# A two-layer feed-forward kernel on one core: the second layer's last token block, its first product run on 256 + 256 or 384 + 128 columns instead of 512

## The chip, the cores and the metric

The kernel runs on one core of a Trainium2 chip. The metric is the device time of one execution in microseconds (us), lower is better. Before the change two executions took 648.00 and 648.39 us, median 648.19 us.

## The reference, cut to what matters

```python
attn_out = _attn_ref(q, k, v, n_sink, window)       # 2 x 8 heads, 768 tokens, 64 wide
x = attn_out.transpose(0, 2, 1, 3).reshape(1536, 512)
# first layer: softplus
h = x @ moe_w_in                                    # 512 -> 2048
x = (np.maximum(h, 0) + np.log1p(np.exp(-np.abs(h)))) @ moe_w_out
# second layer: hard swish
h = x @ moe2_w_in
g = h * np.clip(h + 3.0, 0.0, 6.0) / 6.0
return g @ moe2_w_out                               # 1536 x 512
```

The weights and the attention inputs arrive as 64-bit floats; the result is 32-bit.

## The kernel before

First comes a windowed attention (`banded_attention`, about the first 120 us), which leaves its result transposed in the tile `xT` (128 partitions, a high and a low part, 4 slices of the 512 features, 1536 tokens). Then come the two layers, `w1` (softplus) and `w2` (hard swish). Each layer goes through three token blocks (`blk` 0, 1, 2 of 512 tokens), and each block through 16 slices `c` of 128 hidden features. In all that is 2 x 3 x 16 = 96 steps.

A step has three parts. `products` (lines 136 to 152) makes the tile `h` of one step, 128 hidden features by 512 tokens, in a PSUM tile of pool `psa` (three tiles in turn): for each of the 4 slices of x's features it issues three matrix products, weights high by x high, weights high by x low, weights low by x high, so 12 MATMULs (line 144), each with its own loading of 128 weight columns (LDWEIGHTS, also listed under line 144). `activate` turns h into g; for `w2` that is a Relu on ScalarE (line 178), a product on VectorE (line 180), the high part on ScalarE (line 181) and the low part on VectorE (line 182). `stage_b` (line 201) multiplies g with w_out, again 12 MATMULs in a step (four tiles `y`, three products each), and after the last slice `evac` copies the four y tiles out (lines 218 and 220) and stores them.

All operands of lines 144 and 201 are of the type float32r; the profile prints this type and plain float32 both as "f32" in matrix products. The matrix products of the attention are plain float32: a transposition (lines 525 and 589) shows as one loading and one product, the other ones (lines 483, 552 and 567) as two of each per call in the program. Line 603 are products of zeros in bfloat16 that keep TensorE busy at the start.

`run` issues step s's first products and activation, and then the second product of step s - 2. The first four steps stand in the order in which they are written; from there on (`ffn.run(FIXED, 1000)`) a scheduler sets the order of each engine's instructions, from a model of its own of how long each takes. The second products of the very last two steps are issued tile by tile, each waiting for the one before.

In names of tiles in the rows below the layer's digit is left out: `h_w` is any of `h_w1_...` and `h_w2_...`.

Of the kernel before, what the change touches and what calls it, by code (L numbers as in the profile page):

```python
# [18 lines left out]
P = 128  # L19
# [99 lines left out]
class Ffn:  # L119
# [16 lines left out]
    def products(self, key, blk, c):  # L136
        nc, xT = self.nc, self.xT
        wt = self.w.parts[key, c, 0]
        t0 = blk * 512
        h = self.psa.tile([P, 512], F32, tag="s", name=f"h_{key}_{blk}_{c}")  # L140
        n = 0
        for kk in range(4):
            for ws, xs in ((0, 0), (0, 1), (1, 0)):
                nc.tensor.matmul(  # L144
                    h,
                    wt[:, ws, kk * P : (kk + 1) * P],
                    xT[:, xs, kk, t0 : t0 + 512],
                    start=(n == 0),
                    stop=(n == 11),
                )  # L150
                n += 1
        self.h[key, blk, c] = h

    def activate(self, key, kind, blk, c, filler):
# [641 lines left out]
```

## Time and profile before

| | |
|---|---|
| median of two executions | 648.19 us (648.00 and 648.39) |
| span of the profiled execution, first to last instruction | 646.4 us |
| TensorE busy | 635.6 us, 98% of the span |
| VectorE, ScalarE, GpSimd busy | 335.9, 333.3 and 215.8 us |
| granted TensorE clock, mean over the span | 0.999 of 2.4 GHz |

The profile gives the profiled execution by its span; no separate total is listed for it, so the 1.8 us between the span and the median of the two executions are taken as what lies around it. A busy time counts the stretches in which at least one instruction of an engine was under way. MATMULs overlap, so the time that one costs is the distance from its start to the next start, not the length of its record.

### The profile page before, as it was taken

To read this page: it belongs to the slowest core of one execution; us is meant where nothing else is said; L and a number is where in the kernel's file an instruction comes from. 1 tells how busy PE (TensorE), PEld (TensorE's weight loads), DVE (VectorE), ACT (ScalarE), POOL (GpSimd) and SP (SyncE) were. 2 spreads that over 40 slices of the span, in tenths; PEclk is the share of its full clock that TensorE was granted. 3 is DMA by queue.
4 is the path that set the end of the run, shared out by engine and by line. 5 is a ranking of instruction groups with operands and counts; after the bars stand their busy time and mean duration, and the time that the engine had idled before them with its cause. 6 is when DMAs were issued, how large, how long until landed. Compare 5 with 4: busy or idle time off the path is not lost.

```text
span 646.4 us, 8792 instructions
## 1 busy us (share of the span) xinstructions
PE 635.6 (98%) x3148; PEld 523.0 (81%) x3148; DVE 335.9 (52%) x693; ACT 333.3 (52%) x707; POOL 215.8 (33%) x197
## 2 busy tenths in 40 slices
PE   8999999999999999999999999999999999999996
PEld 4898787878888888888888888888888888888884
DVE  4788989599922422225899987222232222322221
ACT  3777777578866756667777864222222222222221
POOL 1113123489964444445798964000000000000000
PEclk9999999999999999999999999999999999999999
DMA  7744572650000000004665731000010000100001
GB/s 205 236 135 144 164 243 81 233 209 1 1 1 1 0 2 1 1 7 132 189 193 171 219 100 34 1 1 0 2 65 1 0 1 1 65 1 0 1 1 70
DMA packets 38141, 47.06 MB, mean 73 GB/s; under 512 B 2120, under 2 KB 30792, under 8 KB 38088
## 3 DMA queue, kind: packets, MB, share of 16 engines
q1 hardware_dynamic: 37400, 46.15, 22.6%
q8 instruction: 26, 0.43, 0.3%
q10 hardware_dynamic: 688, 0.26, 0.2%
q14 instruction: 27, 0.22, 0.1%
HBM read 43.26 MB, written 3.15 MB: 72 GB/s over the span
## 4 chain that ended last, share of the span: by engine, by line
PE 88%; issue 5%; DVE 3%; ACT 2%; POOL 1%; POOLq 0%; ACTq 0%; DVEq 0%
PE y_w L201 39%; PE h_w L144 39%; PE o L567 3%; PE s L483 2%; PE pt L525 2%; PE spare L603 1%; PE o L552 1%; ACT P L500 1%; POOL w_w L107 1%; DVE xs L495 0%; PE xtr L589 0%; DVE t_w L102 0%; DVE e_w L174 0%; DVE PT L538 0%; POOL ring L460 0%
## 5 line engine op out<-in xcount | busy, mean ns | idle before, releaser
L144 PE MATMUL h_w<-xT,w_w 128*128 128x512 f32 x1152 | 281.9, 389 | 0.8 <-DVE e_w L174 0.8
L144 PEld LDWEIGHTS h_w<-xT,w_w 128*128 128x128 f32 x1152 | 215.9, 188 | 46.7 <-DVE e_w L174 1.3
L201 PE MATMUL y_w<-g_w,w_w 128*128 128x512 f32 x576 | 142.6, 389 | 0.0
L201 PE MATMUL y_w<-w_w,g_w 128*128 128x512 f32 x576 | 138.9, 389 | 0.0
L201 PEld LDWEIGHTS y_w<-w_w,g_w 128*128 128x128 f32 x576 | 108.0, 188 | 23.2 <-ACT g_w L181 0.4
L201 PEld LDWEIGHTS y_w<-g_w,w_w 128*128 128x128 f32 x576 | 108.1, 188 | 22.5
L107 POOL TENSOR_TENSOR w_w<-t_w,w_w 128x512 fp32r<-128x512 f32 x64 | 82.9, 1297 | 44.7 <-ACT w_w L106 44.3
L180 DVE SCALAR_TENSOR_TENSOR h_w<-e_w,h_w 128x512 f32<-128x512 f32 x48 | 33.4, 696 | 89.0 <-ACT e_w L178 89.0
L178 ACT ACTIVATE e_w<-h_w 128x512 f32<-128x512 f32 x48 | 28.7, 599 | 96.2 <-PE h_w L144 94.6
L176 POOL TENSOR_TENSOR g_w<-e_w,g_w 128x512 fp32r<-128x512 f32 x48 | 62.2, 1297 | 43.9 <-ACT g_w L175 43.9
L182 DVE SCALAR_TENSOR_TENSOR g_w<-h_w,g_w 128x512 fp32r<-128x512 f32 x48 | 33.2, 691 | 84.0 <-ACT g_w L181 84.0
L181 ACT ACTIVATE g_w<-h_w 128x512 fp32r<-128x512 f32 x48 | 28.7, 598 | 91.4 <-PE y_w L201 91.1
L170 POOL TENSOR_TENSOR u_w<-u_w,e_w 128x512 f32<-128x512 f32 x48 | 62.1, 1295 | 34.4 <-ACT u_w L169 33.6
L500 ACT ACTIVATE P<-xs,mx 128x272 f32<-128x272 f32 (+1 forms) x96 | 47.3, 494 | 31.8 <-DVE mx L495 31.7
L173 DVE SCALAR_TENSOR_TENSOR h_w<-h_w,r_w 128x512 f32<-128x512 f32 x48 | 33.4, 696 | 58.1 <-ACT r_w L171 58.1
L166 ACT ACTIVATE e_w<-h_w 128x512 f32<-128x512 f32 x48 | 28.4, 592 | 45.5 <-PE h_w L144 39.9
L174 DVE TENSOR_TENSOR e_w<-h_w,u_w 128x512 f32<-128x512 f32 x48 | 33.0, 688 | 28.8 <-POOL u_w L170 28.5
L567 PE MATMUL o<-v,PT 128*128 128x64 f32 x352 | 45.0, 271 | 1.5 <-DVE PT L538 1.3
L106 ACT ACTIVATE w_w<-t_w 128x512 fp32r<-128x512 f32 x64 | 40.0, 625 | 12.6 <-DVE t_w L102 11.7
L567 PEld LDWEIGHTS o<-v,PT 128*128 128x128 f32 x352 | 42.7, 191 | 3.0 <-DVE PT L538 1.9
L96 DVE TENSOR_SCALAR m_w<-raw_w 128x512 int32<-128x512 int32 x52 | 36.1, 693 | 7.5 <-DMA raw_w<-in_moe_w_in_dram 3.6
L175 ACT ACTIVATE g_w<-e_w 128x512 fp32r<-128x512 f32 x48 | 29.9, 624 | 17.4 <-DVE e_w L174 13.6
(80 smaller groups left out, 523.1 us busy)
## 6 DMA issues: line engine op xcount, KB each, us to landing
raw_w<-in_moe_w_in_dram SPq DMA_DIRECT2D x32, 512.0 KB, 5.1
raw_w<-in_moe_w_out_dram SPq DMA_DIRECT2D x32, 512.0 KB, 3.7
v<-in_v_dram SPq DMA_DIRECT2D x12, 256.0 KB, 5.3
out_dram<-o SPq DMA_DIRECT2D x12, 256.0 KB, 2.4
q<-in_q_dram SPq DMA_DIRECT2D x11, 256.0 KB, 3.0
ring<-in_k_dram SPq DMA_DIRECT2D x11, 256.0 KB, 3.8
ring<-in_k_dram ACTq DMA_DIRECT2D x2, 128.0 KB, 6.1
q<-in_q_dram SPq DMA_DIRECT2D x2, 128.0 KB
```

The source lines that it names most:

```text
L96: nc.vector.tensor_scalar(out=m, in0=hi, scalar1=3, scalar2=0x3FFFFFF8, op0=ALU.logical_shift_left, op1=ALU.bitwise_and)
L106: nc.scalar.activation(wt[:, 0, :], t.bitcast(F32), AF.Copy)
L107: nc.gpsimd.tensor_tensor(out=wt[:, 1, :], in0=t.bitcast(F32), in1=wt[:, 0, :].bitcast(F32), op=ALU.subtract)
L144: nc.tensor.matmul(h, wt[:, ws, kk * P : (kk + 1) * P], xT[:, xs, kk, t0 : t0 + 512], start=(n == 0), stop=(n == 11),)
L170: nc.gpsimd.tensor_tensor(out=u, in0=u, in1=e, op=ALU.subtract)
L173: nc.vector.scalar_tensor_tensor(out=h, in0=h, scalar=0.0, in1=r, op0=ALU.max, op1=ALU.add)
L176: nc.gpsimd.tensor_tensor(out=glo, in0=e, in1=ghi.bitcast(F32), op=ALU.subtract)
L180: nc.vector.scalar_tensor_tensor(out=h, in0=e, scalar=6.0, in1=h, op0=ALU.min, op1=ALU.mult)
L182: nc.vector.scalar_tensor_tensor(out=glo, in0=h, scalar=1.0 / 6.0, in1=ghi.bitcast(F32), op0=ALU.mult, op1=ALU.subtract)
L201: ins = nc.tensor.matmul(y, lhsT, rhs, start=(c == 0 and n == 0), stop=(c == 15 and n == 2))
L500: nc.scalar.activation(dst, xs, AF.Exp, scale=-1.0, bias=s["mx"][:, h : h + 1], accum_out=s["sum"][:, h : h + 1])
L567: nc.tensor.matmul(s["o"][:, h, :], t[:, o : o + P], st[gg]["v"][:, h, :], start=(k == 0 and (i <= 1 or hh == 0)), stop=(k == len(blocks) ...
```

## The change

In `products`, for layer `w2` and block 2 alone, the 512 columns (tokens) of a step are cut in two: at 256 where c is even, at 384 where c is odd. For each piece all 12 MATMULs are issued, the second piece after the first; both write into the same PSUM tile. So each of these 16 steps issues 24 MATMULs and 24 loadings instead of 12 and 12, with the same number of columns in sum. Nothing else is edited.

```diff
@@ -138,17 +138,21 @@
         wt = self.w.parts[key, c, 0]
         t0 = blk * 512
         h = self.psa.tile([P, 512], F32, tag="s", name=f"h_{key}_{blk}_{c}")
-        n = 0
-        for kk in range(4):
-            for ws, xs in ((0, 0), (0, 1), (1, 0)):
-                nc.tensor.matmul(
-                    h,
-                    wt[:, ws, kk * P : (kk + 1) * P],
-                    xT[:, xs, kk, t0 : t0 + 512],
-                    start=(n == 0),
-                    stop=(n == 11),
-                )
-                n += 1
+        cuts = (0, 512)
+        if key == "w2" and blk == 2:
+            cuts = (0, 384, 512) if c % 2 else (0, 256, 512)
+        for a, b in zip(cuts, cuts[1:]):
+            n = 0
+            for kk in range(4):
+                for ws, xs in ((0, 0), (0, 1), (1, 0)):
+                    nc.tensor.matmul(
+                        h[:, a:b],
+                        wt[:, ws, kk * P : (kk + 1) * P],
+                        xT[:, xs, kk, t0 + a : t0 + b],
+                        start=(n == 0),
+                        stop=(n == 11),
+                    )
+                    n += 1
         self.h[key, blk, c] = h
```

The order on TensorE, steps 2 and 3 of the block (a row is a call in the program with its count; `h_w_2_3` is h of block 2, slice 3; `y_w_2_0` is its first y tile, fed by the weights and g of the slice named behind the arrow). Before:

```order
L144 MATMUL h_w_2_2_5149<-xT,w_w_2_0_3378 128x512 x12
L144 MATMUL h_w_2_3_5184<-xT,w_w_3_0_3480 128x512
L201 MATMUL y_w_2_0_5168<-w_w_0_1_3268,g_w_2_0_5088 128x512 x3
L144 MATMUL h_w_2_3_5184<-xT,w_w_3_0_3480 128x512
L201 MATMUL y_w_2_1_5172<-w_w_0_1_3268,g_w_2_0_5088 128x512 x3
L201 MATMUL y_w_2_2_5176<-w_w_0_1_3268,g_w_2_0_5088 128x512 x3
L201 MATMUL y_w_2_3_5180<-w_w_0_1_3268,g_w_2_0_5088 128x512 x3
L144 MATMUL h_w_2_3_5184<-xT,w_w_3_0_3480 128x512 x10
```

The same place after the change (line 144 has become 148, line 201 has become 205):

```order
L148 MATMUL h_w_2_2_5173<-xT,w_w_2_0_3378 128x256 x24
L205 MATMUL y_w_2_0_5204<-w_w_0_1_3268,g_w_2_0_5100 128x512 x3
L205 MATMUL y_w_2_1_5208<-w_w_0_1_3268,g_w_2_0_5100 128x512 x3
L205 MATMUL y_w_2_2_5212<-w_w_0_1_3268,g_w_2_0_5100 128x512 x3
L205 MATMUL y_w_2_3_5216<-w_w_0_1_3268,g_w_2_0_5100 128x512 x3
L148 MATMUL h_w_2_3_5220<-xT,w_w_3_0_3480 128x384 x12
L148 MATMUL h_w_2_3_5220<-xT,w_w_3_0_3480 128x128 x12
```

Two products of slice 3 that stood ahead of or between the y products now stand behind them, in one group. This is the only place where the order of groups differs on TensorE before the end of the second layer; on the other engines nothing moved in this stretch.

The end of the layer on TensorE, from the last h on. Before:

```order
L144 MATMUL h_w_2_15_5556<-xT,w_w_15_0_4289 128x512 x12
L201 MATMUL y_w_2_0_5168<-w_w_13_1_4201,g_w_2_13_5507 128x512 x3
L201 MATMUL y_w_2_1_5172<-w_w_13_1_4201,g_w_2_13_5507 128x512 x3
L201 MATMUL y_w_2_2_5176<-w_w_13_1_4201,g_w_2_13_5507 128x512 x3
L201 MATMUL y_w_2_3_5180<-w_w_13_1_4201,g_w_2_13_5507 128x512 x3
L201 MATMUL y_w_2_0_5168<-w_w_14_1_4250,g_w_2_14_5538 128x512 x3
L201 MATMUL y_w_2_0_5168<-w_w_15_1_4297,g_w_2_15_5569 128x512 x3
```

And after:

```order
L148 MATMUL h_w_2_15_5736<-xT,w_w_15_0_4289 128x384 x12
L148 MATMUL h_w_2_15_5736<-xT,w_w_15_0_4289 128x128 x12
L205 MATMUL y_w_2_0_5204<-w_w_13_1_4201,g_w_2_13_5675 128x512 x3
L205 MATMUL y_w_2_1_5208<-w_w_13_1_4201,g_w_2_13_5675 128x512 x3
L205 MATMUL y_w_2_2_5212<-w_w_13_1_4201,g_w_2_13_5675 128x512 x3
L205 MATMUL y_w_2_3_5216<-w_w_13_1_4201,g_w_2_13_5675 128x512 x3
L205 MATMUL y_w_2_0_5204<-w_w_14_1_4250,g_w_2_14_5718 128x512 x3
L205 MATMUL y_w_2_0_5204<-w_w_15_1_4297,g_w_2_15_5761 128x512 x3
```

Here only the pieces of h differ.

## Rows read from the trace of the kernel before

**Rows 1.** The page, busy us (share of the span) and instructions of each engine.

```profile
PE 635.6 (98%) x3148; PEld 523.0 (81%) x3148; DVE 335.9 (52%) x693; ACT 333.3 (52%) x707; POOL 215.8 (33%) x197
```

**Rows 2.** The chain of waits, 547.2 to 632: start us, us, what.

```profile
547.46 2.72 PE h_w L144 x12
550.18 2.72 PE y_w L201 x12
552.90 2.72 PE h_w L144 x12
...
558.34 2.95 PE h_w L144 x13
561.29 0.68 PE y_w L201 x3
561.97 0.23 PE h_w L144
562.20 2.04 PE y_w L201 x9
564.24 2.27 PE h_w L144 x10
...
629.06 2.72 PE h_w L144 x12
```

**Rows 3.** Windows: busy us of each engine in this stretch (instructions), granted clock, DMA.

```profile
547.46:631.78 84.32, 84.32 (x374) 69.82 (x373) 22.81 (x33) 19.75 (x33) 0.00 (x0) 1.00 0.03 13
```

**Rows 4.** Line 144 on PE, 547.4 to 631.6: record ns min/median/max, first and last start.

```profile
L144 PE MATMUL h_w<-xT,w_w x192: 389/389/389, 547.3 to 631.4; 128*128 128x512 f32 x192
```

**Rows 5.** Line 201 on PE, 635.185 to 635.2: the product behind a pause.

```profile
L201 PE MATMUL y_w<-w_w,g_w x1: 499/499/499, 635.2 to 635.2; 128*128 128x512 f32 x1
```

**Rows 6.** Timeline of weight loadings in the attention: start us, us, what.

```profile
71.35 0.97 PEld L567 LDWEIGHTS o<-v,PT 128*128 128x128 f32 x8
```

**Rows 7.** Line 567's loadings, 71.30 to 72.1: record ns min/median/max.

```profile
L567 PEld LDWEIGHTS o<-v,PT x7: 190/192/192, 71.3 to 72.0; 128*128 128x128 f32 x7
```

**Rows 8.** Timeline of PE in the same stretch.

```profile
72.30 0.61 PE L525 MATMUL pt<-ident,P 128*128 128x128 f32 x4
72.74 0.60 PE L589 MATMUL xtr<-ident,x 128*128 128x128 f32 x4
73.18 1.00 PE L567 MATMUL o<-v,PT 128*128 128x64 f32 x8
```

**Rows 9.** Timeline of PE at the start, bfloat16 products at full clock.

```profile
6.65 2.11 PE L603 MATMUL spare<-z 128*128 128x512 bf16 x9
```

**Rows 10.** Who waited for whom, 547 to 632: us in total, times, longest.

```profile
ACT e_w L178 <- PE h_w L144: 34.5, 16, 2.2
ACT g_w L181 <- PE y_w L201: 31.4, 15, 2.5
DVE h_w L180 <- ACT e_w L178: 30.9, 15, 2.1
```

**Rows 11.** Timeline at the end of the layer, 629 to 637.

```profile
631.88 0.60 ACT L178 ACTIVATE e_w<-h_w 128x512 f32<-128x512 f32 x1 [2.18 <-PE h_w L144]
632.51 0.70 DVE L180 SCALAR_TENSOR_TENSOR h_w<-e_w,h_w 128x512 f32<-128x512 f32 x1 [2.09 <-ACT e_w L178]
634.54 0.60 ACT L181 ACTIVATE g_w<-h_w 128x512 fp32r<-128x512 f32 x1 [2.06 <-PE y_w L201]
635.17 0.69 DVE L182 SCALAR_TENSOR_TENSOR g_w<-h_w,g_w 128x512 fp32r<-128x512 f32 x1 [1.96 <-ACT g_w L181]
635.19 0.30 PEld L201 LDWEIGHTS y_w<-w_w,g_w 128*128 128x128 f32 x2 [0.43 <-ACT g_w L181]
635.91 1.23 PEld L201 LDWEIGHTS y_w<-w_w,g_w 128*128 128x128 f32 x6 [0.43 <-DVE g_w L182]
```

## The prediction

> **What bounds the kernel now.** I read the page's first part, then the chain of waits, then the stretch of the change in the windows view, and last the timelines that hold matrix products of other shapes. The page has TensorE busy for 98% of the span, the other engines for at most half [rows 1]. The chain of waits says the same of the last token block of the second layer: from 547.46 to 631.78 us it is nothing but groups of 12 first products (line 144) and 12 second products (line 201), 2.72 us each; where the scheduler mixed two groups (13, 3, 1, 9 and 10 products) the pieces add up to the same [rows 2]. In that stretch TensorE is busy for 84.32 of 84.32 us and its clock is granted in full, 1.00 of 2.4 GHz [rows 3]. So the block is bound by the rate at which TensorE takes pairs of a loading and a product, and what the change does to the time is what it does to that rate.
>
> The rate before: 2.72 us / 12 = 226.7 ns from one pair to the next. 512 columns at 2.4 GHz are 213.3 ns, so a pair costs 13.3 ns more than its columns. That more isn't common to all products: nine bfloat16 products of 512 columns stand 2.11 us from the first start to the last end [rows 9]; less the last one's record of 0.38 us that is eight distances of 216 ns, only 3 ns above the columns.
>
> How long a loading takes when nothing hides it: behind a pause, where loading and product were both let go at 635.19 [rows 11], the product's record is 499 ns long [rows 5], elsewhere 389 in all 192 cases [rows 4]. The difference, 110 ns, is the time in which the product waited for its weights. A product of 512 columns hides that; one of 128 columns can't.
>
> **The change part by part.** It removes 192 pairs of 512 columns (16 steps of 12, 192 in [rows 4]), 43.52 us in sum. It adds, in 8 even steps, 24 pairs of 256 columns each, and in 8 odd steps 12 pairs of 384 and 12 of 128 columns. Columns in sum stay the same; 192 pairs are new.
>
> Pair of 256: columns 106.7 ns; with the 13.3 ns as a cost of each pair 120.0. The loading, 110 ns, just hides behind it. Per even step 24 x 120.0 = 2.880 us, 0.160 more than 2.720; eight steps 1.28 us.
>
> Pair of 384: 160.0 + 13.3 = 173.3 ns, the loading hidden; 12 of them 2.080 us.
>
> Pair of 128: columns 53.3 ns, so the loading should set the distance. Two kinds of row come near. Seven loadings of 128 float32 columns for products with few columns (64) follow each other from 71.35 on: eight in 0.97 us less one record of 0.192 [rows 6, 7], so 0.778 / 7 = 111 ns. Pairs of 128 columns with 128 weight columns (the transpositions) start at 72.30, 72.74 and 73.18, four each, so 110 ns apart [rows 8]. I take 112 ns, the loading's distance rounded up, since there the loading is the longer part as here. 12 x 112 = 1.344 us. An odd step is 2.080 + 1.344 = 3.424 us, 0.704 more; eight steps 5.63 us.
>
> Sum 1.28 + 5.63 = 6.91 us. The bounds of these terms: from below, the 13.3 ns could belong to the columns (1/16 of them) and not to the pair; then 256 costs 113.3, 384 costs 170.0, an even step loses nothing, and with 110 for the narrow pair an odd step loses 0.64 us, in sum 5.1. From above, the 13.3 ns could come on top of the 110 of a loading; then 256 and 128 both cost 123.3, an even step loses 0.24, an odd one 12 x (173.3 + 123.3) - 2720 ns = 0.84 us, in sum 8.6. That the whole record of a loading (192 ns) had to pass between two products is excluded by the 111 ns at which such loadings followed each other [rows 6, 7].
>
> What else moves. The two products of slice 3 that stood between other groups now stand in one piece; in that place TensorE didn't wait [rows 2, 3], so this gains nothing. A longer h reaches ScalarE later, up to 0.7 us, but ScalarE waited 34.5 us for h in this stretch and VectorE 30.9 us for ScalarE [rows 10], and the second product comes two steps later. If that cover were gone, each step would expose the four operations behind h, 0.60 + 0.70 + 0.60 + 0.69 us [rows 11]; it isn't. At the end TensorE pauses twice, 0.43 us on its loadings' row each, for the last g [rows 11]; that chain starts at the last product of the last h, and what TensorE does meanwhile (the 12 second products of slice 13) is unchanged, so both pauses stay. No DMA is added, and no wait.
>
> The profiled span becomes 646.4 + 6.9 = 653.3 us. The runs shown lie 1.8 us above the span, and I leave that as it is: 648.19 + 6.91 = 655.1 us, 1.07% more. A difference of 2% is about what a measurement of this kernel can tell from none, so this counts as within 2%.
>
> **The rivals.** First, loadings that never bind (mechanism: each pair costs its columns plus 13.3 ns, whatever its width). Then 128 costs 66.7, and every step loses 12 x 13.3 = 160 ns, in sum 2.56 us: 650.8 us. For it speaks that one number would explain the 13.3 as a short loading in series with 512 columns; against it the 110 ns behind the pause [rows 4, 5]. The Trainium skill (page "TensorE: Matmul & The Clock Gate", section on weight-path performance modes) has a fast loading, four groups of 32 columns at once, for 128 weights that aren't FP32; by its 32 cycles a loading would be 13.3 ns, and the sum this rival's. Whether float32r counts as FP32 there the page doesn't say; the 110 ns speak for the slow loading.
>
> Second, not slower (mechanism: the 10 ns by which a float32r pair of 512 exceeds a bfloat16 pair arise only in streams as long as 512, where the reads of a loading and of the moving columns meet, and shorter pieces escape it). Place: every pair of the block; price: a piece costs its columns plus 3 ns with its loading hidden. An even step is 24 x 109.8 = 2.63, an odd one 12 x (163.1 + 56.4) = 2.63 us, each 0.09 less than 2.72; in sum 1.4 us gained, 646.8 us. It decides the sign once a narrow pair costs below 66 ns and a wide one below 113. The 216 ns of bfloat16 [rows 9] speak for it, the 111 ns distances of loadings [rows 6] against it. The same page's section on the back-to-back issue gap gives the columns plus 2.5 ns for an isolated product, by which the sum would be this one; it adds that a stream with loadings runs at about 81 ns for 128 columns, by which it would be some 3.9 us of loss. The trace's nearest rows have 110 to 112 ns.
>
> Third, float32r in narrow pieces falls back to the price of plain float32, of which each call shows as two loadings and two products. A pair of 128 then costs 2 x 112 = 224 ns; an odd step is 2.080 + 2.688 = 4.768, 2.05 more; with the even steps 16.4 + 1.3 = 17.7 us, 665.9 us, 2.7% slower. For it: the profile prints both types alike, and no float32r product narrower than 512 stands in the trace. Against it: nothing in the program asks for a second pass.
>
> **How the numbers follow.** The forecast has 0.77, the first rival 0.11, the second 0.03, the third 0.08; 0.01 is for anything else. The likeliest's own range is 653.3 to 656.8 (5.1 to 8.6 us). The range given is 650.3 to 657.5, which takes in the first rival; the second and the third, 0.11 in sum, are left out. The chances: slower by over 2% is the third rival, 0.08; faster by over 2% is none of the cases, 0.01 for the unforeseen; within 2%: 0.91.
>
> **What would show it.** Right: in the chain of waits of the changed kernel, groups of 24 first products of 2.9 us in the even steps; in the odd ones 12 of 2.08 and 12 of 1.34 us; the second products still 2.72; TensorE without idle time in the block; and the end as before, two pauses of 0.43. Wrong: narrow products 67 or 224 ns apart (first and third rival); wide ones at 110 ns (second); a pause of TensorE before a second product, which would mean that the activation's cover was thinner than read; or a clock below 1.00 in the block.

## The result and the profile after

The changed kernel took 655.30 us (median of 655.09 and 655.51), the kernel before 648.19 us: ratio 1.0113, 95% interval [1.0083, 1.0142], so slower by 7.1 us and within 2%. The interval leaves out 1, so here a loss of 1.1% can be told from none, which is finer than the 2% that the prediction names. The forecast was 655.1 us. The profiled span went from 646.4 to 653.7 us.

The page's first part, answering to [rows 1]: busy us (share) and instructions of each engine. TensorE has 192 more products and loadings and 7.0 us more of busy time; the other engines are where they were, to within 1 us.

```profile
PE 642.6 (98%) x3340; PEld 537.6 (82%) x3340; DVE 336.8 (52%) x693; ACT 333.4 (51%) x707; POOL 215.8 (33%) x197
```

The windows view of the changed block, from its first first product to the first second product behind the last h, answering to [rows 3]. The block grew from 84.32 to 91.71 us, by 7.39, which is the whole loss (the span grew by 7.3); TensorE is busy in all of it, at the full clock.

```profile
547.07:638.78 91.71, 91.71 (x566) 84.31 (x565) 22.84 (x33) 19.75 (x33) 0.00 (x0) 1.00 0.03 12
```

The chain of waits in that block, answering to [rows 2]: start us, us, what. The pattern of the first four rows repeats eight times; the last second products stand in a row of 15 with those of the end.

```profile
547.07 2.87 PE h_w L148 x24
549.94 2.75 PE y_w L205 x12
552.69 3.39 PE h_w L148 x24
556.09 2.80 PE y_w L205 x12
558.88 2.87 PE h_w L148 x24
...
635.38 3.39 PE h_w L148 x24
638.78 3.48 PE y_w L205 x15
```

Where the 7.39 us lie: Eight even groups (256 + 256) have 2.87 instead of 2.72: 1.2 us. Eight odd groups (384 + 128) have 3.39 or 3.40: 5.4 us. And the second products, which nobody touched, have 2.75 behind an even group and 2.80 behind an odd one instead of 2.72: 8 x 0.03 + 7 x 0.08 = 0.8 us. Sum 7.4.

Part of that last 0.8 us belongs to the odd groups. The start of a product's record doesn't say that its weights are there: the one behind the pause, let go together with its loading, was 499 ns long instead of 389 [rows 4, 5]. This is the first second product behind a narrow piece (record ns min/median/max):

```profile
L205 PE MATMUL y_w<-w_w,g_w x1: 446/446/446, 555.9 to 555.9; 128*128 128x512 f32 x1
```

It is 57 ns longer than the 389 of an undisturbed one [rows 4]; read in the same way, that is still the wait for its loading, which stands behind the last narrow product. With it, an odd group costs 3.39 + 0.06 = 3.45 us and the second products behind it 2.74, as behind an even group.

The loadings of the narrow pieces, nine that follow each other without a gap in the changed kernel (timeline of loadings), answer to [rows 6]: less one record of 0.192 us [rows 7], 0.888 / 8 = 111 ns apart.

```profile
554.86 1.08 PEld L148 LDWEIGHTS h_w<-xT,w_w 128*128 128x128 f32 x9
```

The view of who waited for whom in the block, answering to [rows 10]: ScalarE waits 41.5 us for h, 7 more than before, VectorE 37.3 us for ScalarE, 6 more. TensorE is never idle here, so it waits for neither of the two.

```profile
ACT e_w L182 <- PE h_w L148: 41.5, 16, 2.9
DVE h_w L184 <- ACT e_w L182: 37.3, 15, 2.8
```

The end of the layer (timeline), answering to [rows 11]: the same two pauses of 0.43 us.

```profile
642.26 0.30 PEld L205 LDWEIGHTS y_w<-w_w,g_w 128*128 128x128 f32 x2 [0.43 <-ACT g_w L185]
642.99 3.03 PEld L205 LDWEIGHTS y_w<-w_w,g_w 128*128 128x128 f32 x14 [0.43 <-DVE g_w L186]
```

### The profile page after: what moved, and what is told of

The parts are those of the page before. It is cut to its first block, busy times and chain, and to the rows that moved or that the text cites. A ratio compares the mean times of both kernels' runs of the same rounds, so it can differ in the third digit from the quotient of the medians.

```text
span 653.7 us, 9176 instructions
## 1 busy us (share of the span) xinstructions
PE 642.6 (98%) x3340; PEld 537.6 (82%) x3340; DVE 336.8 (52%) x693; ACT 333.4 (51%) x707; POOL 215.8 (33%) x197
## 4 chain that ended last, share of the span: by engine, by line
PE 88%; issue 4%; DVE 3%; ACT 2%; POOL 1%; POOLq 0%; ACTq 0%; DVEq 0%
PE h_w L148 39%; PE y_w L205 39%; PE o L571 3%; PE s L487 2%; PE pt L529 2%; PE spare L607 1%; PE o L556 1%; ACT P L504 1%; POOL w_w L107 1%; DVE xs L499 0%; PE xtr L593 0%; DVE t_w L102 0%; DVE e_w L178 0%; DVE PT L542 0%; POOL ring L464 0%
## 5 line engine op out<-in xcount | busy, mean ns | idle before, releaser
L148 PE MATMUL h_w<-xT,w_w 128*128 128x512 f32 (+3 forms) x1344 | 288.3, 362 | 0.8 <-DVE e_w L178 0.8
L148 PEld LDWEIGHTS h_w<-xT,w_w 128*128 128x128 f32 x1344 | 232.8, 189 | 40.4 <-DVE e_w L178 1.2
```

Source lines behind the costliest of these rows:

```text
L148: nc.tensor.matmul(h[:, a:b], wt[:, ws, kk * P : (kk + 1) * P], xT[:, xs, kk, t0 + a : t0 + b], start=(n == 0), stop=(n == 11),)
```

## The experiments

The sum came out, but a sum can come out for wrong reasons: 7.1 us are also 37 ns for each of 192 added pairs. Theory A is the one of the prediction: a pair takes the larger of two things, its columns at 2.4 GHz plus 13.3 ns, or 112 ns, the distance of two loadings of 128 float32 columns. The edits below are to the cut in `products`, for layer w2 and block 2 alone, unless it says otherwise.

**All steps at 256 + 256.**

```diff
-            cuts = (0, 384, 512) if c % 2 else (0, 256, 512)
+            cuts = (0, 256, 512)
```

> All 16 steps cut at 256. Theory A (a pair takes the larger of its columns at 2.4 GHz plus 13.3 ns, and 112 ns, the distance of two loadings): 24 pairs of 120.0 ns a step, 2.88 us in place of 2.72, so 16 x 0.16 = 2.6 us above the kernel before, about 650.8 us. Theory B (every added pair has one price, 7.1 us / 192 = 37 ns, whatever its width): 192 added pairs as in the change, so again 7.1 us, 655.3 us.

Measured: 650.36 us against 648.06 for the kernel before, 2.3 us more, ratio 1.0039 [1.0025, 1.0054]. Its chain of waits repeats these two rows:

```profile
546.93 2.87 PE h_w L148 x24
549.80 2.75 PE y_w L205 x12
```

Theory B, one price for each added pair, is out.

**All steps at 384 + 128.**

```diff
-            cuts = (0, 384, 512) if c % 2 else (0, 256, 512)
+            cuts = (0, 384, 512)
```

> All 16 steps cut at 384. Theory A: 12 x (173.3 + 112) ns = 3.42 us a step, so 16 x 0.70 = 11.3 us above the kernel before, about 659.5 us. Theory B: 192 added pairs, 7.1 us, 655.3 us.

Measured: 659.82 us against 648.06, 11.8 us more, ratio 1.0182 [1.0165, 1.0199]. The same number of pairs as in the experiment above costs five times as much; theory A has it within 0.5 us. Chain of waits:

```profile
547.77 3.40 PE h_w L148 x24
551.17 2.80 PE y_w L205 x12
```

**All steps at 448 + 64: is the narrow pair's price a floor?**

```diff
-            cuts = (0, 384, 512) if c % 2 else (0, 256, 512)
+            cuts = (0, 448, 512)
```

> All 16 steps cut at 448. Theory A, in which the distance of two loadings is a floor that doesn't depend on the columns: narrow pairs again 112 ns apart, wide ones 200.0, so 12 x 312 = 3.74 us a step, 16 x 1.02 = 16.4 us above the kernel before, about 664.6 us. Theory C (a narrow pair costs its columns plus 58.7 ns, which fits 112 at 128 columns): 85 ns for 64 columns, 12 x 285.4 = 3.42 us a step as with 384 + 128, 11.3 us, about 659.5 us. Theory B: 655.3 us.

Measured: 665.70 us against 648.06, 17.6 us more, ratio 1.0276 [1.0255, 1.0296]. Chain of waits:

```profile
547.12 3.69 PE h_w L148 x24
550.81 2.84 PE y_w L205 x12
```

Ten loadings of the narrow pieces, without a gap (timeline of loadings); less one record of 0.192 us, 1.01 / 9 = 112 ns apart:

```profile
556.02 1.20 PEld L148 LDWEIGHTS h_w<-xT,w_w 128*128 128x128 f32 x10
```

64 columns take as long as 128 do: 112 ns. A price of the columns plus something (theory C) is out. The run is 1.2 us above theory A: some 0.5 us is in the first products, whose wide pairs stood 202 ns apart in the trace and not 200.0, and some 0.5 us in the second products behind them (0.03 us a group; 0.02 in the changed kernel).

**All steps at 320 + 192: below 256 columns, but not far.**

```diff
-            cuts = (0, 384, 512) if c % 2 else (0, 256, 512)
+            cuts = (0, 320, 512)
```

> All 16 steps cut at 320. Theory A: 192 columns plus 13.3 are 93.3 ns, below the floor, so 112; 320 are 146.7; 12 x 258.7 = 3.10 us a step, 16 x 0.38 = 6.1 us, about 654.3 us. Theory C: 192 columns cost 80 + 58.7 = 139 ns, 12 x 285.4 = 3.42 us a step, 11.3 us, about 659.5 us. Theory B: 655.3 us.

Measured: 654.32 us against 648.06, 6.3 us more, ratio 1.010 [1.008, 1.012]; theory A has 6.1. Theory B's 7.1 us lie within the interval too, but the runs with 256 + 256 and 384 + 128 exclude it; the chain of waits shows 3.07 us for the 24 pairs, where A has 3.10 and C 3.42.

```profile
547.40 3.07 PE h_w L148 x24
550.48 2.77 PE y_w L205 x12
```

The loadings of the narrow pieces (timeline of loadings) again stand 1.01 / 9 = 112 ns apart:

```profile
554.95 1.20 PEld L148 LDWEIGHTS h_w<-xT,w_w 128*128 128x128 f32 x10
```

So 192 columns cost as much as 128 or 64. By theory A the floor ends where columns plus 13.3 ns make 112, at (112 - 13.3) x 2.4 = 237 columns, an estimate from the distances above.

**384 and 128 alternating: how far ahead do loadings run?** All steps are at 384 + 128, and the loop over the pieces becomes the innermost one; `start` is set at the first product of the tile alone, `stop` at the last. The diff is cut to the loops.

```diff
-        for a, b in zip(cuts, cuts[1:]):
-            n = 0
-            for kk in range(4):
-                for ws, xs in ((0, 0), (0, 1), (1, 0)):
+        n = 0
+        for kk in range(4):
+            for ws, xs in ((0, 0), (0, 1), (1, 0)):
+                for a, b in zip(cuts, cuts[1:]):
```

> All 16 steps cut at 384, the pieces alternating: each of the 12 weight slices is used for 384 and then for 128 columns. Theory A with one loading under way at a time, begun when the product before it begins: the loading behind a narrow product still can't hide, so a narrow and a wide pair together take 285 ns as in the kernel with the pieces one after the other, 11.3 to 11.8 us above the kernel before, about 659.8 us. Theory E (loadings run further ahead, so that only the mean matters: 24 loadings of 112 ns hide behind 12 x (384 + 128) columns): two pairs take 240 ns, 2.6 us above before, about 650.7 us.

Measured: 660.12 us against 648.34, 11.8 us more, ratio 1.0182 [1.0153, 1.0212]: as with the pieces one after the other, and not theory E's 2.6. Chain of waits:

```profile
547.12 3.38 PE h_w L148 x24
550.50 2.81 PE y_w L205 x12
```

A wide product offers more time than one loading needs, but only one loading gets done in it; the one behind the narrow product still waits. So each narrow product costs its 112 ns whatever stands beside it; the mean of the two widths doesn't decide.

**Half the weight columns.** Two kernels that do more work than the reference needs: behind the 12 products of a step (all of 512 columns, as before the change) 12 more write the first 64 rows of h again with the same values.

```diff
+        if key == "w2" and blk == 2:
+            n = 0
+            for kk in range(4):
+                for ws, xs in ((0, 0), (0, 1), (1, 0)):
+                    nc.tensor.matmul(
+                        h[0:64],
+                        wt[:, ws, kk * P : kk * P + 64],
+                        xT[:, xs, kk, t0 : t0 + 512],
+                        start=(n == 0),
+                        stop=(n == 11),
+                    )
+                    n += 1
```

> The kernel before with 12 products added in each of the 16 steps, behind the 12 that are there: half the weight columns (64) by all 512 columns of x, which writes the first half of h once more with the same values. Theory F (the 13.3 ns of a pair belong to its loading and go with its columns): added pairs 213.3 + 6.7 = 220 ns apart, 16 x 12 x 220 = 42.2 us, about 690.3 us. Theory G (they belong to the product): 226.7 ns apart, 43.5 us, about 691.6 us. The distance in the trace decides, the time is too close.

Measured, in one execution: 692.43 us against 648.34, 44.1 us more, so 44.1 / 192 = 230 ns for an added pair. Chain of waits (line 144 the 12 products of before, line 156 the added ones), and below it the records of the added products (ns min/median/max):

```profile
547.40 2.72 PE h_w L144 x12
550.12 2.76 PE h_w L156 x12
```

```profile
L156 PE MATMUL h_w<-xT,w_w x192: 387/391/398, 550.0 to 675.5; 128*64 128x512 f32 x192
```

2.76 / 12 = 230 ns again, so 16.7 more than the columns. Theory F is out at this width: with half the loading the 13.3 ns don't shrink, the pair is even 3 ns slower. Theory G (226.7 ns) is nearer, but the next run goes against it.

The second kernel has the same added products on 128 columns of x:

```diff
-                        h[0:64],
+                        h[0:64, 0:128],
-                        xT[:, xs, kk, t0 : t0 + 512],
+                        xT[:, xs, kk, t0 : t0 + 128],
```

> As e7_weights64, but the added products stream only 128 columns of x. Theory A (the floor of 112 ns is the loading of 128 weight columns): half the weight columns load in about 56 ns, so the added pairs stand 60 to 67 ns apart (53.3 for the columns and 6.7 to 13.3 more), 16 x 12 x 60 to 67 ns = 11.5 to 12.8 us above the kernel before, about 660 us. Theory H (the floor is the rate at which TensorE can be given pairs, whatever they load): 112 ns apart, 21.5 us, about 669.5 us.

Measured: 661.04 us against 648.34, 12.7 us more, ratio 1.0196 [1.0167, 1.0226]. Chain of waits, and below it the loadings' and products' records of line 156 (ns min/median/max):

```profile
549.94 0.72 PE h_w L156 x12
550.66 2.81 PE y_w L213 x12
553.47 2.72 PE h_w L144 x12
```

```profile
L156 PEld LDWEIGHTS h_w<-xT,w_w x192: 134/134/135, 549.6 to 644.2; 128*64 128x64 f32 x192
L156 PE MATMUL h_w<-xT,w_w x192: 220/222/224, 549.8 to 644.2; 128*64 128x128 f32 x192
```

0.72 / 12 = 60 ns a pair: with half the weight columns the 112 ns are gone. So TensorE can be given pairs faster than one in 112 ns (theory H is out), and the floor goes with the 128 weight columns. Half of them also write half the partitions of h, which this edit can't separate; that it is the loading is said by the 110 ns behind the pause, where nothing but a loading stood in the way [rows 5], and by the loadings' records, 134 ns here and 192 for 128 columns.

The 60 ns also say something of the 13.3. A fixed price of a product (theory G) makes 53.3 + 13.3 = 66.7 ns the least for 128 columns, and the pair took 6.7 less. So neither F (230 ns at 512 columns) nor G (60 ns at 128) fits both runs.

No version was faster than the kernel before.

## Why the prediction was right

- **TensorE's rate decides the block.** Held: the block grew by 7.39 us and the span by 7.3 (the block began 0.4 us earlier, and what follows it took 0.3 us more); TensorE was never idle in it.
- **Pair of 256 at 120.0 ns, 1.28 us in all.** Held: 2.87 us for 24, 120 ns each; with all steps cut so 2.3 us in place of 2.6. That the 13.3 ns don't go with the columns is shown by this for 256 of them, since with 1/16 more they would be 113.3. That they are a fixed price of every pair isn't shown: with 64 weight columns it was 16.7 at 512 columns and 6.7 at 128.
- **Pair of 384 at 173.3 and of 128 at 112 ns, 5.63 us in all.** Held: 3.45 us for a group with its last wait, against 3.424. The row chosen for the narrow pair, the loadings of the attention's products with 64 columns [rows 6], fits, since those too stood 111 ns apart; the runs with 448 + 64 and 320 + 192 show the floor at 64 and 192 columns too, and that with half the weight columns shows it gone.
- **Cover of the activation.** Held: ScalarE's wait for h grew by 7.0 us, about as much as the block, so the longer groups of TensorE made ScalarE idle and not the other way round; the two pauses at the end stayed at 0.43 us each.
- **Not in the sum:** the second products behind a piece narrower than 512, of which the prediction said that they stay at 2.72 us. From the end of their first to the end of their last they take 22 ns more per group in the changed kernel (2.515 in place of 2.493 us), about 0.35 us over the block. That explains most of what lies between 6.9 and 7.4 us. Some 0.2 us are in the pieces of 384: in their row of 12 below, 2.27 us less one record of 0.334 make 11 distances of 176 ns and not 173.3. So the block's terms were short by 0.5 us in sum. That the forecast of 655.1 still lies only 0.2 from the 655.3 measured is luck, since two executions of one kernel differ by 0.4 us. The rows below, of the timeline, are the second products before (line 201; the first record is 0.389 us long) and after (line 205; the first record is 0.446 us long), and a row of 384.

```profile
550.02 2.88 PE L201 MATMUL y_w<-w_w,g_w 128*128 128x512 f32 x12
555.92 2.96 PE L205 MATMUL y_w<-w_w,g_w 128*128 128x512 f32 x12
564.34 2.27 PE L148 MATMUL h_w<-xT,w_w 128*128 128x384 f32 x12
```

- **The rivals.** Loadings that never bind (650.8 us) fell with 112 ns for the narrow pair. The Trainium skill (page "TensorE: Matmul & The Clock Gate", section on weight-path performance modes) has a fast loading for weights that aren't FP32; the 32 cycles that the prediction takes from there stand on that page for fp8, as theory. No run here shows a fast loading for float32r, whose loading of 128 columns took 110 ns behind a pause and 111 in a row. The gain (646.8 us) fell with 120.0 ns at 256 columns. The same page of the Trainium skill, section on the back-to-back issue gap, has about 81 ns for a pair with 128 columns in a stream with loadings; here it was 112. Plain float32's price (665.9 us) fell with the same rows: the 8 x 12 narrow products show 96 records, one each, with loadings 111 ns apart.

## What to carry to other kernels

In these runs a float32r product of 128 weight columns paid for its loading unless the product before it lasted longer than the loading, some 112 ns or, as an estimate, about 240 columns. Cut below that, each piece cost the same whatever its width (64, 128 and 192 columns), and a long neighbour didn't help. Above it, every added pair still cost 13 to 16 ns beyond its columns (256 to 448 of them). To price a cut before it is made, look in the trace for the loadings that stand closest to each other, and for a product that follows a pause: what its record is longer than the others' is its wait for the loading.

## What the hardware showed that wasn't expected

With 128 weight columns a float32r pair exceeds its columns by 13 ns at 256, 320 and 512 columns and by some 13 to 16 at 384 and 448, while bfloat16 pairs of 512 have 3 [rows 9]. With 64 weight columns it was 16.7 ns at 512 columns and 6.7 at 128. So it is neither the loading's columns alone nor a fixed price of a product, and what takes it no run here shows.

Also open is why products of 512 columns are slower for a while behind shorter pieces, at full clock and with nothing waited for in the trace. The 11 distances of a group take 2.515 us in place of 2.493, up to 2.523 behind pieces of 64. The excess is in the first half of the group: these are, behind a narrow piece of the changed kernel, the records (ns min/median/max) of the second to the seventh product, and of the last five, which are back at the 389 of before.

```profile
L205 PE MATMUL y_w<-w_w,g_w x6: 387/393/397, 556.2 to 557.4; 128*128 128x512 f32 x6
L205 PE MATMUL y_w<-w_w,g_w x5: 389/389/389, 557.6 to 558.5; 128*128 128x512 f32 x5
```
